# The first superblock's first product done with plain weights, and the combined weights made later

## The chip, the cores and the metric

The kernel runs on one core of a Trainium2 chip. The metric is device time in microseconds: the median of the runs of one build, lower is better. PE is the matrix engine, DVE, ACT and POOL are the vector, scalar and GpSimd engines, and SP issues all DMAs here.

## The reference

Two attentions, then two feed-forward layers over 4608 tokens of width 512, all in fp32. Inner width is 2048.

```python
x = attention(q, packed, packed)            # 4608 x 512, packed = attention(p, k, v)
h = x @ moe_w_in                            # first layer: 512 -> 2048
g = P(h) / (Q(h) + 1e-6)                    # a rational function with |h|
x = g @ moe_w_out                           # 2048 -> 512
h = x @ moe2_w_in                           # second layer: 512 -> 2048
g = h - np.tanh(h)
return g @ moe2_w_out                       # 2048 -> 512
```

## The kernel before

Each fp32 operand of a product is split into a high and a low part (the high part a copy rounded to fp32r, the low part the difference), and a product takes three passes: high x low, low x high, high x high. The weights arrive as 64-bit words and are turned into fp32 on ACT and DVE.

Attention and the first layer run through ten blocks of tokens until about 800 us. The result goes to DRAM as `x2d`. The change concerns the second layer only. There:

- Block 0 (512 tokens) is done plainly. `l3` f (f = 0 to 15) is 12 matmuls 128x512 into one PSUM bank: a slice of 128 of the inner width, from `w3_slot[f]` and the split block `xh`, `xl`. ACT takes tanh (`th`), DVE subtracts (`su`), ACT and DVE split (`yh`, `yl`), and `l4` f adds 12 matmuls with `w4_slot[f]` into four accumulators (f = 15 in four parts, one for each accumulator). Both weights of the layer are loaded during this: a buffer `raw` holds 64-bit words of `w4[f]` and `w3[f + 2]` (two 512 KB loads on SP), DVE and ACT convert them, ACT writes the high part, DVE or POOL the low one. There are two such buffers, so the load for f waits until the conversion for f - 2 is done.
- The other 4096 tokens are four superblocks s = 0 to 3 of 1024 tokens, and these use seven products of half-size blocks in place of eight. The first product of a superblock (`m3`, j = 0 to 7, seven products i of 6 matmuls each, 336 matmuls) needs seven sums or differences of quarters of x (`xa`, and their split `xsh`, `xsl`), and seven combined quarters of the weights. DVE puts its results together (`u2`, `u3`, `h22`, `h21`, `h12`), ACT takes tanh, DVE subtracts (`g11` and so on) and writes the `g` arrays into the slots of `w4`. The second product (`m4`, seven products i of 8 steps, 48 matmuls a product, 336 in all) splits `g` into `yh`, `yl` (`gh` on ACT, `gl` on DVE) for each product.
- The combined weights are made once: for each kind (3 or 4) and j, two sums (`ps`, `prep_sum`), four differences (`pm`, `prep_make`), a split (`ph`, `pl`) into a staging tile `stg` (two of them, which the outputs use too), and a store to DRAM (`pb` stores the three quarters that need no sum, `pd` the four that do). They come back through a ring of four tiles of 8 KB a partition: `load_w3` (`w3d`) and `load_w4` (`w4d`). Two of the ring's tiles are the `raw` buffers, the other two `xh` and `xl` of block 0.

The order is not written out. Every step is entered into a planner (`Plan`) with an engine, a cost, what it needs and a due time, and the planner lists the steps engine by engine. Each engine then runs its list strictly in order, so a step that waits holds up all behind it; that holds for SP's list of DMAs too. A step "EITHER" goes to POOL or DVE.

```python
    order = [(3, j) for j in range(NJ2)] + [(4, j) for j in range(NJ2)]      # L1420
        e = d + (2 * j + 5 if kind == 3 else 2 * j + 14)                     # L1422: due times
        ...
        dma(("pd", kind, j), 128 * 8192, lambda k=kind, j=j: prep_store(k, j), [("pl", kind, j)], e + 0.4)
```

Of the kernel before, what the change touches and what calls it, by code (L numbers as in the profile page):

```python
# [173 lines left out]
def packed_attention_moe_kernel(  # L174
# [555 lines left out]
    w3d = dram_p.tile([NJ2, 128, 7, 2, 256], F32, name="w3d")  # L730
    w4d = dram_p.tile([7, 2, 128, 4, 2, 256], F32, name="w4d")
    x_bufs, xr_t, th_t, yh_t, yl_t, o_t = [], {}, {}, {}, {}, {}
# [6 lines left out]
    def x_load(k):  # L739
        t = yx.tile([128, 512], F32, tag="xr", name="xr", bufs=2)  # L740
        sp.dma_start(out=t, in_=x2d[:, k, 0:NBLK])
        xr_t[k] = t

    def x_high(k):
        act.activation(out=x_bufs[0][:, k, :], in_=xr_t[k], func=AF.Copy)

    def x_low(k, by):
        h, l = x_bufs
        by.tensor_tensor(out=l[:, k, :], in0=xr_t.pop(k), in1=h[:, k, :].bitcast(F32), op=ALU.subtract)

    def hy(f):
        return ps_t[f // 2, "y"][:, f % 2, :]

    def l3(f):
        if f % 2 == 0:
            ring((f // 2, "y"))
        s = w3_slot[f]
        xh, xl = x_bufs
# [7 lines left out]
        for j, (a, b) in enumerate(seq):  # L766
            pe.matmul(out=hy(f), lhsT=a, rhs=b, start=(j == 0), stop=(j == len(seq) - 1))  # L767

    def elem(f, step):
        if step == 0:  # L770
            th_t[f] = yt.tile([128, 512], F32, tag="t", name="t", bufs=TT)
            act.activation(out=th_t[f], in_=hy(f), func=AF.Tanh)
        t = th_t[f]
# [66 lines left out]
    def prep_high(kind, j):  # L840
        s = staged[kind, j] = stg.tile([128, 2048], F32R, tag="stg", name="stg", bufs=2).rearrange(
            "p (part n) -> p part n", part=2)
        act.activation(out=s[:, 0, :], in_=made[kind, j].rearrange("p n f -> p (n f)"), func=AF.Copy)

    def prep_low(kind, j, by):
        s = staged[kind, j]
        by.tensor_tensor(
            out=s[:, 1, :], in0=made[kind, j].rearrange("p n f -> p (n f)"), in1=s[:, 0, :].bitcast(F32), op=ALU.subtract
        )

    def prep_to(kind, j, i):
        if kind == 3:
            return w3d[j][:, ONE.index(i), :, :]
        return w4d[TWO.index(i), j // 4][:, j % 4, :, :]

    def prep_base(kind, j):
        for i, x, half_ in ((1, 0, 0), (2, 0, 1), (3, 1, 1)) if kind == 3 else ((1, 0, 0), (2, 1, 0), (3, 1, 1)):
            s = pair_slot(kind, j, x)[:, 0:1024].rearrange("p (part n) -> p part n", part=2)
            sp.dma_start(out=prep_to(kind, j, i), in_=s[:, :, 256 * half_:256 * half_ + 256].bitcast(F32))

    def prep_store(kind, j):
        s = staged[kind, j]
        for n, i in enumerate(MADE):
            sp.dma_start(out=prep_to(kind, j, i), in_=s[:, :, 256 * n:256 * n + 256].bitcast(F32))

# [3 lines left out]
    def open_ring():  # L869
        ring_w.extend([weights.tile().bitcast(F32R) for _ in range(2)])  # L870
        ring_w.extend(x.rearrange("p k t -> p (k t)") for x in x_bufs)
# [60 lines left out]
    def m3(s, j, i):  # L932
# [128 lines left out]
    add = plan.add  # L1061
# [292 lines left out]
    def open_x():  # L1354
# [3 lines left out]
        x_buf(yx)  # L1358
# [25 lines left out]
    for k in range(4):  # L1384
        e = d - 12 + 2 * k + O("x")
        free = [("xl", k - 2)] if k >= 2 else []
        dma(("xr", k), 512 * 512, lambda k=k: x_load(k), [("open x",)] + reach(0, NBLK) + free, e - 2)
        add(("xh", k), "ACT", c_act(512, 0, 1), lambda k=k: x_high(k), [("xr", k)], e)
        add(("xl", k), EITHER, BOTH, lambda by, k=k: x_low(k, by), [("xh", k)], e, port=True)
# [3 lines left out]

    for f in range(NF):
        e = d + f
        need = [("xl", k) for k in range(4)] if f == 0 else []
# [4 lines left out]
        add(("l3", f), "PE", 12 * MM, lambda f=f: l3(f), need + ago("l3", f, 1), e + P_3, **kw)  # L1401
        add(("th", f), "ACT", AC, lambda f=f: elem(f, 0), [("l3", f), ("open y",)] + ago("yl", f, TT), e + P_E + O("th"))
        add(("su", f), "DVE", AD, lambda f=f: elem(f, 1), [("th", f)], e + P_E)
        add(("yh", f), "ACT", c_act(512, 0, 1), lambda f=f: elem(f, 2), [("su", f)] + ago("l4", f, RING), e + P_E)
        add(("yl", f), "DVE", AD, lambda f=f: elem(f, 3), [("yh", f)], e + P_E, port=True)
# [7 lines left out]
        for m in range(4):  # L1413
# [3 lines left out]
            dma(("os", m), 512 * 512, lambda m=m: o_store(m), [("o", m)], e + P_4)  # L1417


    order = [(3, j) for j in range(NJ2)] + [(4, j) for j in range(NJ2)]  # L1420
    for n, (kind, j) in enumerate(order):
        e = d + (2 * j + 5 if kind == 3 else 2 * j + 14)  # L1422
        was = order[n - 1] if n else None
        after = lambda x: [(x, *was)] if was else []
        have = [("w3" if kind == 3 else "w4", 2 * j + x) for x in range(2)] + [("open y",)]
# [11 lines left out]
        dma(("pb", kind, j), 3 * 128 * 2048, lambda k=kind, j=j: prep_base(k, j), have, e + 0.2)  # L1437
# [3 lines left out]
    def slot_free(kind, f):  # L1441
        return [("l3" if kind == 3 else "l4", f), ("ps", kind, f // 2, f % 2), ("pb", kind, f // 2)]

    add(("ring",), None, 0, open_ring, [("l3", NF - 1)] + [x for y in raw_user[-RAW:] for x in y], 0, behind=raw_next(("ring",)))
    LONG = 28.0
    for s in range(NS):
        base = total + NF + LONG * s
# [3 lines left out]
        for k in range(2):  # L1451
            e = base - 13 + 6 * k
            done = [("xsl", s, i, 0) for i in ONE] if k else last_("xsl", 1, 1) + [("xsl", s - 1, i, 1) for i in ONE] if s else []
            if s == 0 and k == 0:
                done = slot_free(3, 0) + slot_free(3, 1)
            if s == 0 and k == 1:
                done = [("xsl", s, i, 0) for i in ONE]
            dma(("xq", s, k), 2 * 128 * 4096, lambda s=s, k=k: xq_load(s, k), done + reach(T0[s], NSUP), e - 2)
            for n, i in enumerate(XORD):
# [6 lines left out]
                if s == 0:  # L1466
# [5 lines left out]
        for j in range(NJ2):  # L1472
# [175 lines left out]
```

## Time and profile before

| | us |
|---|---|
| median of 3 runs | 1581.49 (1577.44 to 1582.29) |
| profiled execution, its own time | 1585.2 |
| its span, first to last instruction | 1583.4 |
| start of the second layer's first matmul | 781.50 |
| block 0 ends, first superblock starts | 917.38 |
| first superblock's second product starts | 1026.97 |
| second superblock starts | 1109.54 |

The page shows each engine's busy time, then the span in 40 slices of 39.6 us (digits are tenths busy, PEclk is the granted clock of PE in tenths of 2.4 GHz). For this change the second half of the span matters, slices 20 to 28. The stages in the table were read from the timeline of PE; one query gives busy times for each of them. Steps are 1.8 us of the profiled execution outside its span.

### The profile page before, as it was taken

The page shows a single profiled execution, that of the slowest core. Times are in us where ns is not written, and L with a number is a line of the kernel's source. Part 1 is how long each engine was busy: PE and PEld are TensorE (multiplying, and loading weights), DVE is VectorE, ACT ScalarE, POOL GpSimd, SP SyncE. Part 2 cuts the span into 40 slices and gives each one's busy share as a digit, 9 for nine tenths or more (in the row PEclk, how much of TensorE's full clock was granted, in tenths as well). Part 3 has the DMA queues.
Part 4 walks back from the last instruction along what each step waited for, and adds up shares of the span by engine and source line. Part 5 has one row for each costly group of instructions (what it writes and reads, how often), then busy time and mean ns, then how long its engine had stood idle before and what let it go on. Part 6 is the DMA issues. An engine that isn't in the chain of part 4 may idle for free.

```text
span 1583.4 us, 21847 instructions
## 1 busy us (share of the span) xinstructions
PE 1472.3 (93%) x8400; PEld 1196.0 (76%) x8400; DVE 1342.4 (85%) x1738; ACT 887.8 (56%) x1230; POOL 142.7 (9%) x88
## 2 busy tenths in 40 slices
PE   5778999999999999999988766899999999999998
PEld 3657787888888888888966555778778877887787
DVE  4888999999999999999989855997669766967685
ACT  3776676677677676777755522454336433633353
POOL 0101011012110102221111110100000000000000
PEclk9889999999999999999999988999999999999999
DMA  6773313130441213131167999956656755665553
GB/s 239 266 261 142 131 69 124 60 124 31 144 145 61 101 70 117 54 140 67 54 232 244 273 280 295 270 202 231 231 196 227 243 197 192 221 229 187 195 196 142
DMA packets 91575, 272.54 MB, mean 172 GB/s; under 512 B 7888, under 2 KB 46928, under 8 KB 76624
## 3 DMA queue, kind: packets, MB, share of 16 engines
q1 hardware_dynamic: 91472, 271.16, 50.7%
q8 instruction: 66, 1.08, 0.3%
q14 instruction: 37, 0.30, 0.1%
HBM read 218.70 MB, written 52.43 MB: 171 GB/s over the span
## 4 chain that ended last, share of the span: by engine, by line
PE 66%; DVE 18%; DMA 5%; ACT 5%; issue 3%; POOL 1%; SPq 0%; DVEq 0%; ACTq 0%; POOLq 0%
PE acc L964 19%; PE acc L656 16%; PE h L964 15%; PE h L643 9%; PE h L767 2%; DMA raw<-in_w_dram 2%; PE h L509 2%; DVE gh L698 1%; DVE yl L1007 1%; DVE t L685 1%; DVE gl L707 1%; DVE m L704 1%; DVE m L700 1%; DVE t L681 1%; DVE slot L521 1%
## 5 line engine op out<-in xcount | busy, mean ns | idle before, releaser
L643 PE MATMUL h<-ah,slot 128*128 128x320 f32 (+3 forms) x1024 | 214.9, 304 | 1.2 <-DVE slot L521 1.2
L656 PE MATMUL acc<-gh,slot 128*128 128x512 f32 (+1 forms) x800 | 178.0, 376 | 10.9 <-DVE slot L1206 10.4
L656 PEld LDWEIGHTS acc<-gh,slot 128*128 128x128 f32 x800 | 149.5, 195 | 35.7 <-DVE slot L1206 12.2
L643 PEld LDWEIGHTS h<-ah,slot 128*128 128x128 f32 x1024 | 170.7, 193 | 2.6 <-DVE slot L521 1.4
L656 PE MATMUL acc<-raw,slot 128*128 128x512 f32 (+1 forms) x720 | 164.6, 379 | 0.0
L643 PE MATMUL h<-al,slot 128*128 128x192 f32 (+3 forms) x512 | 151.1, 309 | 8.0 <-DVE slot L521 2.3
L656 PEld LDWEIGHTS acc<-raw,slot 128*128 128x128 f32 x720 | 130.2, 188 | 31.8 <-issue 10.5
L1003 ACT ACTIVATE yh<-slot 128x512 fp32r<-128x512 f32 x140 | 87.3, 631 | 79.7 <-PE acc L964 31.2
L678 POOL TENSOR_TENSOR m<-u,r 128x1024 f32<-128x1024 f32 (+1 forms) x33 | 72.5, 2198 | 483.4 <-ACT r L674 381.9
L1007 DVE TENSOR_TENSOR yl<-slot,yh 128x512 fp32r<-128x512 f32 x140 | 95.6, 691 | 21.7 <-ACT yh L1003 20.7
L643 PEld LDWEIGHTS h<-al,slot 128*128 128x128 f32 x512 | 98.4, 192 | 18.0 <-DVE slot L521 2.6
L670 ACT ACTIVATE u<-h 128x1024 f32<-128x1024 f32 (+1 forms) x80 | 74.6, 932 | 60.4 <-PE h L643 60.1
L986 ACT ACTIVATE t<-slot 128x512 f32<-128x512 f32 x60 | 37.9, 632 | 110.6 <-DVE slot L979 65.2
L964 PE MATMUL h<-slot,raw 128*128 128x512 f32 x336 | 81.5, 398 | 18.8 <-DVE slot L981 15.6
L681 DVE TENSOR_TENSOR t<-t,h 128x1024 f32<-128x1024 f32 (+1 forms) x80 | 88.3, 1106 | 9.1 <-ACT t L666 8.8
L666 ACT ACTIVATE t<-h,coa 128x1024 f32<-128x1024 f32 (+1 forms) x80 | 89.4, 1120 | 11.2 <-PE h L643 6.3
L656 PE MATMUL acc<-gl,slot 128*128 128x384 f32 (+1 forms) x400 | 93.0, 374 | 2.1 <-DVE gl L707 2.0
L685 DVE SCALAR_TENSOR_TENSOR t<-t,coa,h 128x1024 f32<-128x1024 f32 (+1 forms) x80 | 93.3, 1166 | 1.9 <-ACT u L670 1.2
L690 ACT ACTIVATE r<-m,lnb 128x1024 f32<-128x1024 f32 (+1 forms) x60 | 63.6, 1059 | 53.2 <-POOL m L678 36.8
L964 PEld LDWEIGHTS h<-slot,raw 128*128 128x128 f32 x336 | 63.1, 190 | 35.8 <-DVE slot L981 16.1
L964 PE MATMUL acc<-yh,raw 128*128 128x512 f32 x288 | 88.8, 389 | 0.0
L656 PEld LDWEIGHTS acc<-gl,slot 128*128 128x128 f32 x400 | 71.3, 190 | 21.4 <-issue 8.2
(192 smaller groups left out, 3255.0 us busy)
## 6 DMA issues: line engine op xcount, KB each, us to landing
raw<-in_w_dram SPq DMA_DIRECT2D x64, 512.0 KB, 5.4
w<-w1d SPq DMA_DIRECT2D x28, 1024.0 KB, 4.8
raw<-w4d SPq DMA_DIRECT2D x28, 1024.0 KB, 4.9
raw<-w3d SPq DMA_DIRECT2D x16, 1024.0 KB, 5.3
xh<-w3d SPq DMA_DIRECT2D x16, 1024.0 KB, 5.1
xh<-w4d SPq DMA_DIRECT2D x14, 1024.0 KB, 4.8
xl<-w4d SPq DMA_DIRECT2D x14, 1024.0 KB, 5.3
raw<-w3d SPq DMA_DIRECT2D x16, 768.0 KB, 4.4
```

The source lines that it names most:

```text
L643: pe.matmul(out=ps[:, f, t], lhsT=x, rhs=y, start=(i == 0), stop=(i == len(seq) - 1))
L656: pe.matmul(out=acc_t[n][m][:, 0:XW[n]], lhsT=w2_slot[2 * p + f][:, o:o + 128], rhs=x[:, f, :], start=(p == 0 and part == 512 and f == 0), ...
L666: act.activation(out=t_t[g], in_=hv(g), func=AF.Identity, scale=a3, bias=a2)
L670: act.activation(out=u_t[g], in_=hv(g), func=AF.Abs)
L678: by.tensor_tensor(out=q_m[g], in0=u_t.pop(g), in1=r_t[g], op=ALU.mult)
L681: dve.tensor_tensor(out=t_t[g], in0=t_t[g], in1=hv(g), op=ALU.mult)
L685: dve.scalar_tensor_tensor(out=t, in0=t, scalar=a1, in1=hv(g), op0=ALU.add, op1=ALU.mult)
L690: act.activation(out=r, in_=q_m[g], func=AF.Ln, scale=2.0 ** -LN_SHIFT, bias=lnb[:, 0:1])
L964: pe.matmul(out=to, lhsT=a, rhs=b, start=(first and n == 0 and i in (1, 6, 7, 5)), stop=(last and n == len(seq) - 1), skip_group_check=True,)
L986: act.activation(out=t, in_=b["a"] if what == "t11" else g_of(what[1:], j), func=AF.Tanh)
L1003: act.activation(out=yh_t[s, i, f], in_=g_of(GSRC[i], f), func=AF.Copy)
L1007: by.tensor_tensor(out=yl_t[s, i, f], in0=g_of(GSRC[i], f), in1=yh_t[s, i, f].bitcast(F32), op=ALU.subtract)
```

## The change

Of the first superblock, the first product is now done plainly: `l3` runs for three blocks b = 0, 1, 2 of 512 tokens (b = 1 and 2 are the two halves of superblock 0). For b = 1 and 2, `su` writes straight into the `g` arrays (`g11`, `g12`, `g21`, `g22`; free once the weights of that slot are used, summed and stored), and only `s3` is left of the putting together. Block 1's split x takes the two `raw` buffers, block 2's takes those of block 0. The second product `m4` of superblock 0 stays as it was. Its combined weights (kind 4) are made first, but not before `w4[14]` is there, from j = 1 on not before `w4[15]`; the weights for `m3` (kind 3) follow, and are first used by superblock 1. `w3d` is a plain row of 3584 words a partition in the order 1, 2 (high then low of the pair), 6, 7, 5, 4, 3: stored with rows of 4 KB (the first slot), 8 KB (the four made) and twice 1 KB, in 3 DMAs a j where there were 7. The staging tile holds high and low of one quarter side by side, so the four stores of kind 4 have rows of 2 KB where they had twice 1 KB. The loads of the ring are chained in their order of use (`stream`).

```diff
-    w3d = dram_p.tile([NJ2, 128, 7, 2, 256], F32, name="w3d")
+    w3d = dram_p.tile([NJ2, 128, 3584], F32, name="w3d")
...
-    def x_buf(where):
-        x_bufs.extend(where.tile([128, 4, 512], F32R, tag=f"x{x}0", name=f"x{x}0") for x in "hl")
+    def x_buf(b):
+        if b == 1:
+            x_bufs[b] = [weights.tile().bitcast(F32R).rearrange("p (k t) -> p k t", k=4) for _ in range(2)]
+        else:
+            x_bufs[b] = x_bufs[0] if b else [yx.tile([128, 4, 512], F32R, tag=f"x{x}0", name=f"x{x}0") for x in "hl"]
...
         if step == 1:
-            dve.tensor_tensor(out=t, in0=hy(f), in1=t, op=ALU.subtract)
-            if f % 2:
-                ps_t.pop((f // 2, "y"))
+            to = g_of(f"{b}{f % 2 + 1}", f // 2) if b else t
+            dve.tensor_tensor(out=to, in0=hy(b, f), in1=t, op=ALU.subtract)
...
+    def prep_store(kind, j):
+        s = staged[kind, j].bitcast(F32)
         if kind == 3:
...
+            sp.dma_start(out=w3d[j][:, 1024:3072], in_=s.rearrange("p n part f -> p (n part f)"))
+            return
         for n, i in enumerate(MADE):
...
+    IN_W3 = {1: (0, 0, 512), 2: (0, 256, 768), 6: (0, 1024, 1280), 7: (0, 1536, 1792),
+             5: (1, 0, 256), 4: (1, 512, 768), 3: (1, 1024, 1280)}
...
+    def base_free(b, f):
+        x = f - f % 2 + b - 1
+        return [("l4", x), ("ps", 4, x // 2, 0), ("ps", 4, x // 2, 1), ("pb", 4, x // 2, x % 2)]
...
+    for b in range(1, 3):
+        for f in range(NF):
+            e = d + (16.5 if b == 1 else 24.5) + 0.5 * f
...
+            add(("l3", b, f), "PE", 12 * MM, lambda b=b, f=f: l3(b, f), need, e, **kw)
...
+            add(after_su(b, f), "DVE", AD, lambda b=b, f=f: elem(b, f, 1), [("th", b, f)] + base_free(b, f), e + 0.5)
...
-    order = [(3, j) for j in range(NJ2)] + [(4, j) for j in range(NJ2)]
+    AFTER, LATE = 14, 8
+    order = [(4, j) for j in range(NJ2)] + [(3, j) for j in range(NJ2)]
     for n, (kind, j) in enumerate(order):
-        e = d + (2 * j + 5 if kind == 3 else 2 * j + 14)
+        e = d + (2 * j + 5 if kind == 4 else j + 24)
...
-        have = [("w3" if kind == 3 else "w4", 2 * j + x) for x in range(2)] + [("open y",)]
+        have = [("w3" if kind == 3 else "w4", 2 * j + x) for x in range(2)] + [("w4", min(NF - 1, 2 * j + AFTER) if kind == 4 else NF - 1)] + [("open y",)]
...
-        for j in range(NJ2):
+        for j in range(NJ2) if s else ():
             e = base + 1.75 * j
```

What this does to the lists, at three places. First SP, from the last store of x of the first layer on. Before (`raw<-in_w_dram` are the weight loads, `slot<-x2d` loads x for superblock 0, `w3d<-` are stores of combined weights):

```order
L720 DMA x2d<-q 128x2x384 x2
L859 DMA w3d<-slot_88 128x2x256 x2
L859 DMA w3d<-slot_89 128x2x256
L326 DMA raw<-in_w_dram 128x512
L892 DMA slot_6882<-x2d 128x1024
L892 DMA slot_6883<-x2d 128x1024
L864 DMA w3d<-stg 128x2x256 x4
L326 DMA raw<-in_w_dram 128x512 x2
L859 DMA w3d<-slot_90 128x2x256 x2
```

After, from the same store on (`xr` are the two tiles through which block 1's x is loaded):

```order
L720 DMA x2d<-q 128x2x384 x2
L326 DMA raw<-in_w_dram 128x512 x18
L863 DMA w4d<-slot_74 128x2x256
L863 DMA w4d<-slot_75 128x2x256 x2
L326 DMA raw<-in_w_dram 128x512
L871 DMA w4d<-stg 128x512 x4
L863 DMA w4d<-slot_955 128x2x256
L863 DMA w4d<-slot_1084 128x2x256
L744 DMA xr<-x2d 128x512 x2
```

Eighteen weight loads now stand in one piece; the stores of combined weights begin behind them. Second PE, at the end of block 0. Before, the last `l4` (into `acc`) and then `m3` of superblock 0, whose weights are in `raw`:

```order
L797 MATMUL acc_6899<-yl,ex_6817 128x512
L798 MATMUL acc_6899<-yh,ex_6817 128x512
L799 MATMUL acc_6899<-yh,ex_6817 128x512
L964 MATMUL h<-slot_7038,raw 128x512 x2
L964 MATMUL h<-slot_7305,raw 128x512 x2
```

After, `l4` of f = 13 and then `l3` of block 1, whose x is in `raw` (slot_88 holds w3[0]):

```order
L800 MATMUL acc_6891<-yl,ex_6819 128x512
L801 MATMUL acc_6891<-yh,ex_6819 128x512
L802 MATMUL acc_6891<-yh,ex_6819 128x512
L770 MATMUL h<-raw,slot_88 128x512 x12
L770 MATMUL h<-raw,slot_89 128x512 x12
```

All 16 of block 1 and two of block 2 stand ahead of `l4` of f = 14; the last six matmuls of `l4` stand behind block 2. Third DVE, early in `m4` of superblock 0. Before (`yl<-` is `gl`, L999 are sums of `g`, L906 and L918 belong to x of superblock 1):

```order
L918 TENSOR_TENSOR slot_7253<-slot_6883,slot_7253 128x512
L1007 TENSOR_TENSOR yl<-slot_7663,yh 128x512
L999 TENSOR_TENSOR slot_7663<-slot_7663 128x512
L999 TENSOR_TENSOR slot_7677<-slot_7663,slot_7677 128x512
L1007 TENSOR_TENSOR yl<-slot_7772,yh 128x512
```

After (L833, L841 and L850 are `ps`, `pm` and `pl` of kind 3):

```order
L1020 TENSOR_TENSOR yl<-slot_7930,yh 128x512
L833 TENSOR_TENSOR s_8288<-slot_70 128x512
L850 TENSOR_TENSOR stg<-made,stg 128x4x256
L833 TENSOR_TENSOR s_8303<-slot_71 128x512
L1020 TENSOR_TENSOR yl<-slot_7965,yh 128x512
L841 TENSOR_TENSOR made<-s_8303,s_8288 128x256
```

The making of the last combined weights of kind 3 has moved in between the splits of `g`.

## Rows read from the trace of the kernel before

**Rows 1.** The page: span, PE, and its slices of granted clock and DMA share.

```profile
span 1583.4 us, 21847 instructions
PE 1472.3 (93%) x8400; PEld 1196.0 (76%) x8400; DVE 1342.4 (85%) x1738; ACT 887.8 (56%) x1230; POOL 142.7 (9%) x88
...
PEclk9889999999999999999999988999999999999999
DMA  6773313130441213131167999956656755665553
```

**Rows 2.** Busy times by stage of the second layer, with the columns in the first line.

```profile
core 0: us, PE busy (x) PEld busy (x) DVE busy (x) ACT busy (x) POOL busy (x), PEclk, DMA share, GB/s
781.50:809.73 28.23, 21.42 (x106) 18.60 (x105) 22.51 (x26) 17.73 (x25) 4.66 (x4) 0.98 0.49 169
809.73:917.38 107.65, 89.54 (x336) 68.57 (x336) 97.61 (x149) 55.80 (x81) 16.08 (x14) 0.91 0.88 273
917.38:1026.97 109.59, 84.22 (x337) 65.73 (x337) 71.85 (x115) 36.02 (x56) 13.44 (x14) 0.88 0.94 278
1026.97:1109.54 82.57, 78.92 (x337) 64.09 (x336) 67.87 (x110) 41.01 (x69) 0.00 (x0) 0.98 0.62 220
1109.54:1583.40 473.86, 468.25 (x2017) 376.78 (x2015) 352.59 (x556) 195.59 (x328) 0.00 (x0) 1.00 0.59 204
```

**Rows 3.** Timeline of PE: start, length, instruction, idle time before it and what ended it.

```profile
809.73 0.77 PE L767 MATMUL h<-xh,slot 128*128 128x512 f32 x1 [6.28 <-DVE t L775]
...
818.05 0.39 PE L797 MATMUL acc<-yl,slot 128*128 128x512 f32 x1
...
932.57 0.80 PE L964 MATMUL acc<-slot,xh 128*128 128x512 f32 x1 [4.88 <-DVE o L810]
...
992.42 2.93 PE L964 MATMUL h<-slot,raw 128*128 128x512 f32 x6 [15.64 <-DVE slot L981]
...
1036.22 0.47 PE L964 MATMUL h<-yl,xl 128*128 128x512 f32 x1 [3.65 <-DMA xl<-w4d]
```

**Rows 4.** Timeline of SP's queue, weight loads and what stands between them.

```profile
796.71 0.81 SPq L326 DMA_DIRECT2D raw<-in_w_dram  x2
...
807.88 0.62 SPq L326 DMA_DIRECT2D raw<-in_w_dram  x1
811.15 1.03 SPq L892 DMA_DIRECT2D slot<-x2d  x2
...
819.19 1.00 SPq L326 DMA_DIRECT2D raw<-in_w_dram  x2
...
852.34 0.82 SPq L326 DMA_DIRECT2D raw<-in_w_dram  x2
...
860.19 0.82 SPq L326 DMA_DIRECT2D raw<-in_w_dram  x2
```

**Rows 5.** Timelines of ACT and POOL: first and last step of one buffer's conversion.

```profile
801.64 1.18 ACT L350 ACTIVATE raw<-raw 128x1024 f32<-128x1024 f32 x1 [5.75 <-DMA raw<-in_w_dram]
...
806.26 1.29 POOL L1206 TENSOR_TENSOR slot<-raw,slot 128x512 fp32r<-128x512 f32 x1 [2.73 <-DVE slot L1206]
```

**Rows 6.** Timeline of DVE where it runs without a gap.

```profile
1002.90 1.23 DVE L847 TENSOR_TENSOR stg<-made,stg 128x1024 fp32r<-128x1024 f32 x1
1004.04 0.69 DVE L979 TENSOR_TENSOR ex<-acc,u 128x512 f32<-128x512 f32 x1
1004.64 0.68 DVE L981 TENSOR_TENSOR ex<-acc,u 128x512 f32<-128x512 f32 x1
...
1006.43 0.42 DVE L838 TENSOR_TENSOR made<-s 128x256 f32<-128x256 f32 x1
1006.77 0.69 DVE L983 TENSOR_TENSOR ex<-acc,u 128x512 f32<-128x512 f32 x1
```

**Rows 7.** DMA view of 824 to 832 us, where only combined weights are stored.

```profile
DMA packets 2792, 2.93 MB, mean 367 GB/s; under 512 B 170, under 2 KB 2711, under 8 KB 2792
```

More of the change, by code (lines that the diff above doesn't have):

```diff
@@ L841, in prep_high @@
         s = staged[kind, j] = stg.tile([128, 2048], F32R, tag="stg", name="stg", bufs=2).rearrange(
[L842 to L843 removed]
+            "p (n part f) -> p n part f", n=4, part=2)
+        act.activation(out=s[:, :, 0, :], in_=made[kind, j], func=AF.Copy)
     def prep_low(kind, j, by):
         s = staged[kind, j]
[L847 to L849 removed]
@@ L851, in prep_to @@
-    def prep_to(kind, j, i):
-        if kind == 3:
[L853 to L859, printed above, removed]
@@ L861, in prep_store, with prep_base @@
-    def prep_store(kind, j):
-        s = staged[kind, j]
+        by.tensor_tensor(out=s[:, :, 1, :], in0=made[kind, j], in1=s[:, :, 0, :].bitcast(F32), op=ALU.subtract)
+    def prep_base(kind, j, x):
+        s = pair_slot(kind, j, x)[:, 0:1024].bitcast(F32)
+        if kind == 3 and x == 0:
+            sp.dma_start(out=w3d[j][:, 0:1024], in_=s)
+            return
+        s = s.rearrange("p (part n) -> p part n", part=2)
+        for i, half_ in [(3, 1)] if kind == 3 else [(2, 0), (3, 1)] if x else [(1, 0)]:
+            if kind == 3:
+                to = w3d[j][:, 3072:3584].rearrange("p (part n) -> p part n", part=2)
+            else:
+                to = w4d[TWO.index(i), j // 4][:, j % 4, :, :]
+            sp.dma_start(out=to, in_=s[:, :, 256 * half_:256 * half_ + 256])
@@ L863, in prep_store @@
+    def prep_store(kind, j):
+        s = staged[kind, j].bitcast(F32)
+        if kind == 3:
+            sp.dma_start(out=w3d[j][:, 1024:3072], in_=s.rearrange("p n part f -> p (n part f)"))
+            return
         for n, i in enumerate(MADE):
-            sp.dma_start(out=prep_to(kind, j, i), in_=s[:, :, 256 * n:256 * n + 256].bitcast(F32))
+            sp.dma_start(
+                out=w4d[TWO.index(i), j // 4][:, j % 4, :, :].rearrange("p a f -> p (a f)"),
+                in_=s[:, n, :, :].rearrange("p a f -> p (a f)"),
+            )
@@ L1357, in open_x @@
         yx = pool_of(last, "yx", side="right")
-        x_buf(yx)
+        x_buf(0)
     def open_y():
@@ L1383, in packed_attention_moe_kernel @@
     d = total
[L1384 to L1389, printed above, removed]
+    add(("open x", 1), None, 0, lambda: x_buf(1), [x for y in raw_user[-RAW:] for x in y], 0, behind=raw_next(("open x", 1)))
@@ L1394, in packed_attention_moe_kernel @@
     for f in range(NF):
         e = d + f
-        need = [("xl", k) for k in range(4)] if f == 0 else []
+        need = [("xl", 0, k) for k in range(4)] if f == 0 else []
         need += [("w3", f)]
@@ L1436, in packed_attention_moe_kernel, with stream @@
             [("ph", kind, j)], e + 0.3, port=True)
-        dma(("pb", kind, j), 3 * 128 * 2048, lambda k=kind, j=j: prep_base(k, j), have, e + 0.2)
+        for x in range(2):
+            dma(("pb", kind, j, x), (1 + (x if kind == 4 else 1 - x)) * 128 * 2048, lambda k=kind, j=j, x=x: prep_base(k, j, x), have, e + 0.2 + x * LATE)
         dma(("pd", kind, j), 128 * 8192, lambda k=kind, j=j: prep_store(k, j), [("pl", kind, j)], e + 0.4)
     def slot_free(kind, f):
-        return [("l3" if kind == 3 else "l4", f), ("ps", kind, f // 2, f % 2), ("pb", kind, f // 2)]
-    add(("ring",), None, 0, open_ring, [("l3", NF - 1)] + [x for y in raw_user[-RAW:] for x in y], 0, behind=raw_next(("ring",)))
+        return [("l3", 2, f) if kind == 3 else ("l4", f), ("ps", kind, f // 2, f % 2), ("pb", kind, f // 2, f % 2)]
     LONG = 28.0
+    streamed = []
+    def stream(name, *a, **kw):
+        dma(name, *a, take="w", behind=streamed[-1:], **kw)
+        streamed.append(name)
     for s in range(NS):
-        base = total + NF + LONG * s
+        base = total + NF + (LONG * s + 2 if s else 0)
         last_ = lambda x, *k: [(x, s - 1, *k)] if s else []
-        for k in range(2):
+        for k in range(2) if s else ():
             e = base - 13 + 6 * k
[L1453 to L1456, printed above, removed]
+            if k:
                 done = [("xsl", s, i, 0) for i in ONE]
+            else:
+                done = [("xsl", s - 1, i, 1) for i in ONE] if s > 1 else slot_free(3, 0) + slot_free(3, 1)
             dma(("xq", s, k), 2 * 128 * 4096, lambda s=s, k=k: xq_load(s, k), done + reach(T0[s], NSUP), e - 2)
@@ L1569, in packed_attention_moe_kernel @@
                     if i in (7, 5):
-                        need += [(x, s, NJ2 - 1) for x in ("g11", "u2", "h21", "h12")]
+                        need += [(x, s, NJ2 - 1) for x in ("g11", "u2", "h21", "h12")] if s else [("o", m) for m in range(4)]
                     need += {2: [("mp1", s, 0), ("mp1", s, 1)], 4: [("mu3", s, 0), ("mu3", s, 1)],
```

138 lines of the change are left out of this document (78 added, 60 removed).

## The prediction

> **What bounds the kernel now.** I read the page first. PE is busy 93% of the span, so in general the kernel is bound by PE; but its granted clock dips from 9 to 8 tenths, after the kernel's first slices, only in the 24th and 25th, and the DMA share in the 23rd to 26th is 9 tenths where it is 5 to 7 nearly all the time behind [rows 1]. That is the stretch the change touches. The table by stage then shows what a matmul costs when nothing disturbs PE: 473.86 us for the 2016 matmuls of superblocks 1 to 3, or 0.235 us each, at a granted clock of 1.00 (the upper level, 2.4 GHz) [rows 2]. Against this price the stages of the change lose time. `m3` of superblock 0 takes 109.59 us where 336 x 0.235 = 79.0 would do; the rest of block 0 (809.73 to 917.38) loses about 35 us in the same way; `m4` takes 82.57 and loses 3.6 [rows 2]. So there are about 66 us ahead of 1026.97 that are not matmul work.
>
> The timeline of PE says what ends these waits: 4.88 us for an `o` copy on DVE, 15.64 us for a `u` or `h` result on DVE at 992.42, 3.65 us for a ring load at the start of `m4` [rows 3]. DVE is busy 97.61 of 107.65 us in block 0 [rows 2]: it makes the combined weights there, the `raw` conversions and the elementwise work. The DMA runs at shares of 0.88 and 0.94, 273 and 278 GB/s, in the two stages [rows 2]. So block 0 and `m3` are bound by DVE and by transfers, in turns, and PE waits at a granted clock of 0.91 and 0.88, below full. From 1109.54 on nothing waits.
>
> **The change part by part.** I use the profiled execution: its time is 1585.2 us, and the median of the runs is 1581.49, 3.7 less. The stretch to price runs from 818.05, where PE does the first matmul of `l4` of f = 0 [rows 3], to 1109.54.
>
> *Loads of the weights.* Stores and loads of x leave the front of SP's list, and eighteen 512 KB loads stand in one piece. Before, the third pair did not go out together: one load at 807.88, the second at 819.19 behind `x2d` and stores [rows 4]. What sets the pace now is the buffer: load issued at 796.71, conversion from 801.64 on ACT, low part done on POOL at 806.26 + 1.29 = 807.55 [rows 4, 5], so 10.8 us a buffer and, with two buffers, 5.4 us a pair. PE needs two groups of 12 for each f, 2 x 12 x 0.235 = 5.64 us. Both are about the same, so PE becomes the pace. Block 1's first group stands behind `l3` of f = 15 and `l4` of f = 13. From 818.05 that is 24 groups (14 of `l4`, 10 of `l3`), 24 x 12 x 0.235 = 67.7 us: `l3` of block 1 starts at 885.7. The other bound is the pace of before, 852.34 to 860.19 = 7.85 us a pair [rows 4]; five to six more pairs at 2.2 us above 5.64 put this point at about 899. I take 885.7, since the stores that slowed the pace have left SP's list there.
>
> *Matmuls.* Superblock 0's first product has 2 x 16 x 12 = 384 matmuls in place of 336. The 48 more cost 48 x 0.235 = 11.3 us, all on PE's path. Two groups of `l4` (24 matmuls) also lie behind 885.7. (384 + 24) x 0.235 = 95.9 us.
>
> *Waits in this stretch.* The sums `xa`, the splits `xsh` and `xsl`, the results `u2` to `h12` of superblock 0 and their 15.64 us wait go. What is late next: DVE still makes all of kind 4 while PE runs `l3`. `su` may write a `g` array only after the kind 4 store of that slot has read it, so a `g` waits for SP and DMA. Per j, kind 4 puts 7 x 2 x 128 x 256 x 4 B = 1.835 MB on the queues; at before's 278 GB/s this takes 6.6 us against the 5.64 in which PE does one pair of `l3`. With eight j this is at most 8 x 1 = 8 us, and PSUM and `t` tiles take up a part. I take 4 us, with 0 to 12 as bounds: 0 if the stores keep up, 12 if the last store also delays the loads of `m4`.
>
> *Handing over to `m4`.* The last `l4` and `s3`, `gh`, `gl` stand ahead of the first matmul. Before, PE waited 3.65 us for a ring load here [rows 3]. I take 2.5, bounds 1.5 to 5.
>
> *`m4` of superblock 0.* It took 82.57 us with DVE busy 67.87 [rows 2]. DVE now also makes the combined weights of kind 3 there, and loses nothing in return except copies that went earlier. I count 116 steps on half-tiles, 12 on quarters and 4 splits of 128x1024. In the gapless stretch one step starts 0.60 us after another for 128x512, 0.34 us for 128x256 and 1.14 us for the split (1004.04 to 1004.64; 1006.43 to 1006.77; 1002.90 to 1004.04) [rows 6]. 116 x 0.60 + 12 x 0.34 + 4 x 1.14 = 78.3 us. PE needs 336 x 0.235 = 79.0. I leave 82.6 as before; bounds 79 and 90 (the full durations 0.69, 0.42 and 1.23 [rows 6] give 90).
>
> *Transfers.* From 861, where the last weights of w4 that the stores wait for are converted, to the end of `m4`: 14.7 MB of stores of kind 4, 14.7 of kind 3, 14.7 of loads of kind 4, 3.7 of x for block 2 and superblock 1, 1.0 of output, 0.5 of the last `raw`, 3.7 for the first loads of kind 3: 53.0 MB. To finish by 1070.7 they need 253 GB/s. The two stages before got 273 and 278 [rows 2], so this is covered, by little.
>
> *Longer rows.* Kind 3 goes out in 3 DMAs a j where there were 7. With 0.82 us for two issues [rows 4] this saves SP 8 x 4 x 0.41 = 13 us of issuing, but SP has nothing waiting behind it that PE waits for; I count it at nothing, and 13 us late stores if that cover is gone. Whether longer rows move bytes faster is not shown directly. In the stretch where only combined weights are stored, 2,711 of 2,792 packets are under 2 KB and yet 367 GB/s move [rows 7]. The mixed stage has 278 GB/s at a share of 0.94, 296 at full share; the steady stage, which only loads long rows, has 204 at 0.59, 346 at full share [rows 2]. So I put the gain at zero, with 53.0 MB in 153 rather than 179 us (346 against 296 GB/s) as the other end; it would matter only if transfers bound the stretch.
>
> The Trainium skill, "DMA: Bandwidth & Descriptors", section on specifications, says that transfers of 512 B or more run at line rate; by it the longer rows of this change bring nothing. The 367 GB/s with short packets [rows 7] agree with it, the 296 against 346 do not clearly. By either, the sum stays as it is.
>
> *The sum.* 885.7 + 95.9 + 4 + 2.5 + 82.6 = 1070.7 for the end of `m4`, against 1109.54: 38.8 us less. Superblocks 1 to 3 keep their 473.9 us. The profiled execution would be 1585.2 - 38.8 = 1546.4, the median 1581.49 - 38.8 = 1542.7.
>
> **The rivals.** *Transfers and loads keep their pace of before.* `l3` of block 1 starts at 899, the stretch waits 8 us, handing over 2.5, and `m4` takes 86 as DVE gets late: 899 + 95.9 + 8 + 2.5 + 86 = 1091.4, a gain of 18, or 1563. For it speaks that DMA shares were 0.88 and 0.94 [rows 2]; against it, that POOL and ACT had room (16 and 56 us of 108 [rows 2]) and the stores moved behind the loads.
>
> *Starved by transfers, slower.* All 53 MB fall in one stretch, loads of `m4` behind the stores on the same list. The point from which it decides is 53.0 MB / (1109.54 - 861) = 213 GB/s. At 190 GB/s the transfers take 279 us, `m4` ends at 1140, and the time is about 1612. The stretch of before with both loads and stores gave 273 [rows 2], so it would need a worse mixture; the steady stage's 204 GB/s is at a share of 0.59 only [rows 2], thus no limit.
>
> *The wait moves (no change).* Kind 3 is made so late that superblock 1 waits for it: each `w3d` row must be stored before it is loaded. Making one j is about 8 steps on DVE, 2 x 0.60 + 4 x 0.34 + 1.14 = 3.7 us; four of eight lie in `m4`. If DVE pushed these behind its `gl` work, superblock 1 would wait for up to 8 x 3.7 = 30 us plus a store and a load, and about 35 of the 38.8 would be given back: 1578. Against it: 78.3 of 82.6 us fit.
>
> **How the numbers follow.** Forecast 0.69, transfers and pace as before 0.22, starved 0.05, wait moves 0.04. The predicted time is the forecast's, 1543. Low: all good bounds (no waits, 1.5, 79.0) give 885.7 + 95.9 + 1.5 + 79 = 1062, a gain of 47, 1534, and as the runs scatter by 4 us, and longer rows could give some, 1528. High: the rival at 1563 and a little above, 1568; all bad bounds together (899 + 95.9 + 12 + 5 + 90 = 1102) would give 1574. What lies outside are the starved and moved cases and the far end of the second. A measurement of this kernel can tell 0.3%, 4.7 us, from no change. Faster by more: 0.91; within: 0.03; slower: 0.06.
>
> **What would show it.** In the profile of the changed kernel: `l3` of block 1 starts near 886, pairs of `raw` loads 5.4 to 5.7 us apart, the granted clock near 1.0 between 818 and 985; `m4` starts near 988 and ends near 1071; DMA at 253 GB/s or more between 861 and 1071; DVE without gaps in `m4`; superblocks 1 to 3 in 158 us each. Wrong it would be if PE waits for `su` (a store too late), for `w4d` at the start of `m4`, or for `w3d` in superblock 1.

## The result, and the profile after

| | before | after |
|---|---|---|
| median, us | 1579.61 (1577.44 to 1582.29, 4 runs) | 1538.57 (1534.80 to 1540.94, 4 runs) |
| profiled execution, span | 1583.4 | 1534.7 |
| `l4` of f = 0 starts | 818.05 | 814.44 |
| `l3` of block 1 starts (before: block 0 ends) | 917.38 | 880.81 |
| `m4` of superblock 0 starts | 1026.97 | 978.69 |
| superblock 1 starts | 1109.54 | 1061.19 |

The ratio is 0.9737, 95% interval 0.9707 to 0.9767: 41.0 us faster. Forecast were 38.8 us less and 1543, with 1528 to 1568 as range.

The page of the changed kernel first, its counterpart is [rows 1]. The fence shows span and PE, then granted clock and DMA share in 40 slices.

```profile
span 1534.7 us, 21747 instructions
PE 1462.3 (95%) x8448; PEld 1194.2 (78%) x8448; DVE 1307.3 (85%) x1690; ACT 878.3 (57%) x1216; POOL 135.2 (9%) x82
...
PEclk8888999999999999999999999999999999999999
DMA  7783314221332303132134696776656655665553
```

PE runs 48 matmuls more than before and is busy 10 us less. The two slices with a clock of 8 tenths in the second half are gone, and only one slice has a DMA share of 9 tenths where there were four. The stages, one row each (rest of block 0; from `l3` of block 1 to `m4`; `m4`; the three other superblocks), with the columns of [rows 2] and against its rows:

```profile
807.48:880.81 73.33, 73.33 (x312) 59.65 (x313) 58.31 (x85) 43.74 (x65) 11.84 (x9) 0.98 0.54 185
880.81:978.69 97.88, 94.21 (x410) 76.35 (x408) 66.20 (x111) 34.12 (x52) 8.83 (x12) 1.00 0.78 263
978.69:1061.19 82.50, 79.64 (x337) 62.44 (x338) 77.75 (x130) 45.70 (x75) 1.30 (x1) 1.00 0.73 269
1061.19:1534.70 473.51, 468.24 (x2017) 376.76 (x2015) 352.45 (x556) 195.42 (x328) 0.00 (x0) 1.00 0.60 207
```

In block 0, PE is busy in every one of the 73.33 us: the 18 us of waits are gone, and the granted clock is 0.98 where it was 0.91. In the second row 3.67 us are idle, in `m4` 2.86, where DVE is now busy 77.75 of 82.50 us. The last row is that of before to 0.4 us. So the whole gain lies in block 0 and the first product, as forecast. PE's timeline has these waits behind 880 us (the two ahead of `m4`; seven more in it, of 0.15 to 0.67 us, make up the 2.86; in brackets the idle time and what ended it):

```profile
935.83 0.50 PE L770 MATMUL h<-xh,slot 128*128 128x512 f32 x1 [1.63 <-DVE ex L779]
978.69 0.50 PE L977 MATMUL h<-yl,raw 128*128 128x512 f32 x1 [2.04 <-DVE yl L1020]
```

The waits of 15.64 and 4.88 us in [rows 3] have no successor.

### The profile page after: what moved, and what is told of

Its sections match the earlier page's. It is cut to its first block, busy times and chain, and to the rows that moved or that the text cites. A ratio compares the mean times of both kernels' runs of the same rounds, so it can differ in the third digit from the quotient of the medians.

```text
span 1534.7 us, 21747 instructions
## 1 busy us (share of the span) xinstructions
PE 1462.3 (95%) x8448; PEld 1194.2 (78%) x8448; DVE 1307.3 (85%) x1690; ACT 878.3 (57%) x1216; POOL 135.2 (9%) x82
## 4 chain that ended last, share of the span: by engine, by line
PE 68%; DVE 21%; ACT 5%; issue 3%; DMA 2%; POOL 1%; SPq 0%; DVEq 0%; ACTq 0%; POOLq 0%
PE acc L977 17%; PE acc L656 16%; PE h L977 12%; PE h L643 9%; PE h L770 9%; DVE yl L1020 2%; PE h L509 2%; DVE t L685 1%; DMA raw<-in_w_dram 1%; DVE gh L698 1%; DVE t L681 1%; DVE gl L707 1%; DVE m L704 1%; DVE m L700 1%; DVE slot L1012 1%
## 5 line engine op out<-in xcount | busy, mean ns | idle before, releaser
L656 PEld LDWEIGHTS acc<-gh,slot 128*128 128x128 f32 x800 | 149.5, 195 | 36.0 <-DVE slot L1219 12.8
L1020 DVE TENSOR_TENSOR yl<-slot,yh 128x512 fp32r<-128x512 f32 x140 | 95.5, 693 | 15.6 <-ACT yh L1016 14.8
L770 PE MATMUL h<-xh,slot 128*128 128x512 f32 x256 | 83.9, 399 | 8.0 <-DVE t L779 6.4
L1016 ACT ACTIVATE yh<-ex 128x512 fp32r<-128x512 f32 x84 | 52.6, 631 | 50.6 <-PE acc L977 25.5
L977 PE MATMUL acc<-yh,raw 128*128 128x512 f32 x256 | 78.9, 389 | 0.0
L999 ACT ACTIVATE t<-slot 128x512 f32<-128x512 f32 x45 | 28.5, 633 | 85.8 <-DVE slot L992 48.8
```

Source lines behind the costliest of these rows:

```text
L656: pe.matmul(out=acc_t[n][m][:, 0:XW[n]], lhsT=w2_slot[2 * p + f][:, o:o + 128], rhs=x[:, f, :], start=(p == 0 and part == 512 and f == 0), ...
L770: pe.matmul(out=hy(b, f), lhsT=a, rhs=w, start=(j == 0), stop=(j == len(seq) - 1))
L977: pe.matmul(out=to, lhsT=a, rhs=b, start=(first and n == 0 and i in (1, 6, 7, 5)), stop=(last and n == len(seq) - 1), skip_group_check=True,)
L1016: act.activation(out=yh_t[s, i, f], in_=g_of(GSRC[i], f), func=AF.Copy)
L1020: by.tensor_tensor(out=yl_t[s, i, f], in0=g_of(GSRC[i], f), in1=yh_t[s, i, f].bitcast(F32), op=ALU.subtract)
```

## The experiments

Stage lengths come from each run's own trace: A from the first `l4` to the first `l3` of block 1, B from there to `m4`, C is `m4`. A of the changed kernel holds 288 matmuls, B 408. In no_hold, plain_early, make_extra and store_extra, 24 matmuls of `l4` (some 5.5 us) stand in A instead of B.

| run | A | B | C | median, us |
|---|---|---|---|---|
| changed kernel | 66.37 | 97.88 | 82.50 | 1538.57 |
| after_again | 66.38 | 97.87 | 82.55 | 1538.26 |
| short_rows | 66.37 | 97.88 | 82.53 | 1539.96 |
| no_hold | 92.30 | 88.49 | 77.78 | 1552.21 |
| plain_early | 89.08 | 110.18 | 77.24 | 1565.76 |
| make_extra | 91.12 | 103.18 | 83.06 | 1568.84 (one run) |
| store_extra | 92.54 | 94.99 | 83.63 | 1564.41 (one run) |
| hold_alone (A to `m3`, B is `m3`) | 78.25 | 142.75 | 83.74 | 1596.37 |
| fewer | 66.34 | 81.84 | 82.52 | 1523.42 |
| double | 66.35 | 110.19 | 82.54 | 1552.61 |
| l4_early | 66.37 | 95.99 | 83.07 | 1538.49 |
| spread | 66.35 | 96.00 | 80.53 | 1534.53 |
| hold12 | 70.60 | 102.54 | 84.02 | 1546.80 |

**The same kernel again.** 

> The changed kernel itself once more, beside the next runs. Time 1535 to 1541 as before. If the 2.3 us by which the first layer ended earlier in the first trace (second layer from 779.2 instead of 781.5) belong to one execution only, this trace shows another start; if the change itself moved the first layer, it shows 779 again.

Ratio 0.9731 (0.9707 to 0.9754). Here the second layer starts at 783.67, in the first trace at 779.20; the stages behind differ by at most 0.05 us. So the stages can be compared to a tenth of a microsecond, while the time of a run cannot: of the 5.0 us between the two profiled executions, 4.5 lie ahead of the second layer.

**Longer rows.** The stores go back to 1 KB rows (`stg` holds high and low apart again), seven DMAs a j:

```diff
-            sp.dma_start(out=w3d[j][:, 1024:3072], in_=s.rearrange("p n part f -> p (n part f)"))
-            return
...
         for n, i in enumerate(MADE):
...
+            sp.dma_start(out=prep_to(kind, j, i), in_=s[:, :, 256 * n:256 * n + 256].bitcast(F32))
```

> The changed kernel with the stores of before: seven DMAs a j with rows of twice 1 KB for both kinds, everything else as in the changed kernel. The prediction's step (longer rows count at nothing): 1536.5 to 1540.5, l3 of block 1 from about 881, m4 ends at about 1061. Rival, rows gave the transfers their room (53 MB in 153 instead of 179 us, 13 us of SP issuing): PE waits for su behind late stores or for the ring loads of m4, 1545 to 1565.

Ratio 0.9741 (0.9718 to 0.9764), and the stages are equal. Stage B of this run, with the columns of [rows 2], is:

```profile
888.00:985.88 97.88, 94.22 (x410) 76.35 (x408) 66.18 (x111) 34.26 (x52) 8.86 (x12) 1.00 0.83 263
```

The same 263 GB/s take a DMA share of 0.83 with short rows and 0.78 with long ones. So long rows do save DMA time, 6% of it here, but nothing waits for it: they are worth nothing in this kernel. The Trainium skill, "DMA: Bandwidth & Descriptors", section on specifications, has all transfers from 512 B on at line rate; for the time of the kernel that came out, for the DMA engines' own share it is not quite so.

**No hold.** Kind 4 is made as soon as its slots are there:

```diff
-... + [("w4", min(NF - 1, 2 * j + AFTER) if kind == 4 else NF - 1)] + [("open y",)]
+... + ([("w4", NF - 1)] if kind == 3 else []) + [("open y",)]
```

> The changed kernel, but kind 4 is made as soon as its own two slots are there, not after w4[14] and w4[15]; its stores stand between the weight loads again. The prediction's step (stores behind the loads let the loads keep PE's pace): pairs of loads 7 to 8 us apart for five to six pairs, l3 of block 1 starts 8 to 14 us later (889 to 895), 1546 to 1553. Rival, the plain product alone took the waits away: l3 of block 1 at 881, 1536 to 1541.

Ratio 0.9815 (0.9791 to 0.9840). The time is where it was expected, 14 us above the changed kernel, but it comes about in another way. A grows by 26 us, 20 without the matmuls that moved there, where 8 to 14 were expected; B is shorter by 9, of which 5.5 are these matmuls, and C by 4.7: DVE makes no combined weights there, and 12 of its steps on x of superblock 1 fall into `m4` instead of 21. SP's timeline shows where the loads stop (the `raw` loads are the weight loads):

```profile
806.85 2.71 SPq L326 DMA_DIRECT2D raw<-in_w_dram  x3
...
818.28 1.80 SPq L871 DMA_DIRECT2D w4d<-stg  x4
...
830.25 0.81 SPq L326 DMA_DIRECT2D raw<-in_w_dram  x2
```

SP stands for 8 us ahead of a store whose tile is still being made, and no weight load leaves for 20 us. It looks as if the store held up the loads; make_extra below, which has no such store, shows the same pause, so the store is not its cause.

**Plain product alone.** Neither kind is held, and kind 3 is made ahead of kind 4 with the due times of before:

```diff
-    order = [(4, j) for j in range(NJ2)] + [(3, j) for j in range(NJ2)]
+    order = [(3, j) for j in range(NJ2)] + [(4, j) for j in range(NJ2)]
-        e = d + (2 * j + 5 if kind == 4 else j + 24)
+        e = d + (2 * j + 5 if kind == 3 else 2 * j + 14)
...
-        have = [... for x in range(2)] + [("w4", min(NF - 1, 2 * j + AFTER) if kind == 4 else NF - 1)] + [("open y",)]
+        have = [... for x in range(2)] + [("open y",)]
```

> The plain product alone: the changed kernel, but the combined weights are made in the order and at the due times of before (kind 3 first, then kind 4, each as soon as its slots are there). The theory that the plain product and the later making are both needed: the weight loads go at 7 to 8 us a pair again, and the g arrays of block 1 wait for kind 4, which now comes last; 1550 to 1575. Rival, the plain product alone is the cause: 1537 to 1545.

Ratio 0.9889 (0.9868 to 0.9910). A is 3 us shorter than in no_hold, and B now has 13.94 us of PE waits, nearly all for `su` (5.83 and 4.11 us the longest), which stands on DVE behind the making of kind 4 or waits for a store of it to leave a `g` slot. C is 77.24 us, with no wait at all. The plain product without the new order is worth 1.1%, that is 17 of the 41 us.

**Later making alone.** The kernel before, with the hold:

```diff
-        have = [... for x in range(2)] + [("open y",)]
+        have = [... for x in range(2)] + [("w4", min(NF - 1, 2 * j + 14) if kind == 3 else NF - 1)] + [("open y",)]
```

> The later making alone: the kernel before, with its m3 of superblock 0, but kind 3 is not made before w4[14] or w4[15] is there and kind 4 not before w4[15]. Block 0 then ends near 892 instead of 917, but m3 of superblock 0 waits for kind 3: its first load comes only after the first making and a store, and DVE has sums, splits, results and the making in it. The theory that moving needs the plain product as cover: what block 0 gains m3 gives back, 1570 to 1600. Rival, moving alone is the cause: 1540 to 1558.

Ratio 1.0079 (1.0056 to 1.0102), 0.8% slower. Block 0 gets 21 us shorter (78.25 against 99.33), and `m3` 33 us longer. In PE's timeline, then ACT's:

```profile
909.91 2.07 PE L964 MATMUL h<-slot,raw 128*128 128x512 f32 x4 [14.14 <-DVE slot L918]
...
947.03 1.22 PE L964 MATMUL h<-slot,raw 128*128 128x512 f32 x2 [33.15 <-DVE slot L918]
```

```profile
944.06 1.06 ACT L843 ACTIVATE stg<-made 128x1024 fp32r<-128x1024 f32 x1 [23.80 <-DMA out_dram<-o]
```

PE waits for the split of x (L918). The first of the two splits waits for a load of x that SP issues only at 899.96, among the stores of kind 3. The second stands behind the making, which waits 23.80 us for a staging tile: block 0's output, held in it, is stored by SP behind some thirty stores that the hold had let go together. So this order of the lists is slow; a better one for the same idea was not tried.

**Making or storing.** What in the early making stretches A? Two runs took it apart. In make_extra kind 4 is made once more in block 0 (as a kind 5, into the same tiles), and nothing of it is stored:

```diff
-    order = [(4, j) for j in range(NJ2)] + [(3, j) for j in range(NJ2)]
+    order = [(5, j) for j in range(NJ2)] + [(4, j) for j in range(NJ2)] + [(3, j) for j in range(NJ2)]
```

> What stretched block 0 when kind 4 was made early (92.3 us from the first l4 to l3 of block 1 instead of 66.4, 5.5 of it for two groups of l4 more): the making itself on DVE, ACT and POOL, or its stores. Here the changed kernel makes kind 4 once more in block 0, as soon as the slots are there, and stores nothing of that; the weight loads stay in one piece on SP's list. If the making alone did it: 75 to 87 us from the first l4 to l3 of block 1. If the stores did it, by their bytes or by standing ahead of loads in SP's list: 66 to 69.

In store_extra seven pieces of each pair of slots are stored to a spare place, and nothing is made:

```diff
+    for j in range(NJ2):
+        dma(("extra", j), 7 * 128 * 2048, lambda j=j: extra_store(j), [("w4", 2 * j), ("w4", 2 * j + 1)], d + 2 * j + 5)
```

> The counterpart: the changed kernel stores seven 256 KB pieces of each pair of w4 slots to a spare place in block 0, as soon as the slots are there, 14.7 MB in all, without any making. The stores stand between the weight loads, but wait for no making. If bytes or queue places are what stretched block 0: 75 to 87 us from the first l4 to l3 of block 1. If it takes stores that wait for the making ahead of loads on SP's list: 66 to 70.

Each alone stretches A about as much as both together: 91.12 and 92.54 against 92.30. Both expectations that left one of them out fell. A of no_hold, of make_extra, then of store_extra:

```profile
818.79:911.09 92.30, 79.49 (x313) 62.22 (x312) 71.42 (x111) 46.41 (x67) 13.76 (x12) 0.93 0.78 250
```

```profile
816.13:907.25 91.12, 78.32 (x311) 61.31 (x309) 69.86 (x107) 45.24 (x66) 14.65 (x12) 0.94 0.36 123
```

```profile
817.90:910.44 92.54, 78.41 (x314) 61.64 (x313) 55.00 (x72) 39.68 (x59) 13.94 (x11) 0.93 0.67 216
```

In no_hold it was the making. In make_extra no store stands between the loads until 878 us, and yet the loads pause for the same 20 us, from 806.6 to 826.89. SP's timeline, and DVE's with the last step of a conversion (the low part, L1219), read:

```profile
803.19 3.40 SPq L326 DMA_DIRECT2D raw<-in_w_dram  x3
...
826.89 20.84 SPq L326 DMA_DIRECT2D raw<-in_w_dram  x8
```

```profile
826.14 1.28 DVE L1219 TENSOR_TENSOR slot<-raw,slot 128x512 fp32r<-128x512 f32 x2
```

The load leaves when the first of these two low parts is done, at about 826.8; in no_hold the same step starts at 829.51 and the load leaves at 830.25, though SP has had nothing to issue since 827.7. PE's longer waits in A are the same one by one too, 1.25, 0.60, 1.79, 2.28, 0.92 and 5.45 us in make_extra, 1.24, 0.60, 1.81, 2.29, 0.92 and 5.45 in no_hold. So in A the stores cost no_hold at most the 1.2 us between the two. The waits of 5.45 us are for a `yl` that stands on DVE behind sums of the making and splits of x, the others for converted weights.

store_extra has a path of its own: its stores stand between the loads and wait for the slots that they store. But not all of its 92.54 us is their price. The load of `w4[15]` leaves at 897.52, behind stores of the first quarters that kind 4 makes itself: SP waits for these from 891.25 to 894.57 and issues them until 897.43, some 6 us in all. In the changed kernel the load leaves ahead of them. PE's longest wait there, 8.23 us, is for these weights. That stores alone cost as much as the making is therefore not shown.

No engine is full in make_extra, and DMA is at 0.36. What is full is the cycle of the two load buffers: load, conversion on ACT and DVE, low part, next load. The first step of a conversion on ACT, for f = 5 and f = 13, in the changed kernel and in make_extra:

```profile
810.91 1.13 ACT L350 ACTIVATE raw<-raw 128x1024 f32<-128x1024 f32 x1
...
854.44 1.17 ACT L350 ACTIVATE raw<-raw 128x1024 f32<-128x1024 f32 x1 [0.32 <-POOL slot L1219]
```

```profile
810.12 1.17 ACT L350 ACTIVATE raw<-raw 128x1024 f32<-128x1024 f32 x1
...
883.30 1.13 ACT L350 ACTIVATE raw<-raw 128x1024 f32<-128x1024 f32 x1
```

That is (854.44 - 810.91) / 8 = 5.44 us a pair of loads, and 9.15 in make_extra. The kernel before has 8.97 by the same rows (818.80 and 890.57), no_hold 8.30, store_extra about 8.0. What was queued between the steps of this cycle, the making on ACT, DVE and POOL or the stores on SP, lengthened it. PE then waits, and runs at a granted clock of 0.93 to 0.94: in no_hold, 12.8 us of A are waits and about 7.6 are matmuls that take longer (79.49 us for 313, against 66.37 for 289).

**What is next to PE.** Four of twelve matmuls are left out of each group of block 1 and 2, so that the result lacks one pass there:

```diff
+        if b:
+            seq = [x for n, x in enumerate(seq) if n % 2 == 0 or n >= 8]
```

> The changed kernel without the pass high x low (xl) in block 1 and 2: four matmuls of each of the 32 groups are left out, 128 in all. If PE is the bound of this stretch, with 0.23 us a matmul, 29 us go: 1508 to 1511. If the transfers set it next (25 MB between 881 and 977, at 296 GB/s 85 us) only about 11 go: 1526 to 1530. If DVE or the waits for stores do, somewhere between.

Ratio 0.9620 (0.9600 to 0.9639), 1523.42: between the bounds for PE and for the transfers, as expected if DVE or the waits for stores come next. B falls by 16 us where PE has 29 us less to do. From 900 to 924 us the row of the changed kernel and of this run are:

```profile
900.00:924.00 24.00, 24.00 (x108) 19.87 (x107) 21.88 (x37) 10.11 (x13) 4.42 (x6) 1.00 1.06 324
```

```profile
900.00:924.00 24.00, 18.40 (x70) 13.79 (x69) 22.59 (x39) 11.30 (x17) 4.65 (x7) 0.93 1.02 307
```

In the changed kernel PE, DVE (21.88 of 24 us) and DMA (share 1.06, 324 GB/s) are all full there. With less on PE, the other two stay full and PE waits for `su` (9.5 us in B; 2.03 more are for the first `yl` of `m4`). This run does not tell which of the two comes next.

**More stores.** The made quarters of kind 4 are stored twice:

```diff
+        for n, i in enumerate(MADE):
+            sp.dma_start(out=w4x[TWO.index(i), j // 4][:, j % 4, :, :]..., in_=s[:, n, :, :]...)
```

> The changed kernel, but each of the 32 stores of the four made quarters of kind 4 is issued twice, the second time to a spare place: 8.4 MB and 32 DMAs more, most of them between 868 and 925. If 296 GB/s is the limit of a mixed stretch, the 33 MB up to 977 take 113 instead of 96 us: 10 to 18 us more, 1549 to 1557. If the transfers have room (367 GB/s in a stretch of stores alone): 0 to 4 us more, 1538 to 1543.

Ratio 0.9805 (0.9785 to 0.9825): B is 12.3 us longer, with 11.4 us of waits, 8.8 of them for `su`. B moves 302 GB/s, more than the 296 that had been worked out as a limit from stages with more loads, and 385 in a part with stores alone (924 to 940). At the 324 GB/s above, 8.4 MB would take 26 us, so about half was hidden. The time fits the first expectation, its limit was somewhat low. The copies also put 32 more issues on SP's list, some 13 us at 0.41 us each, which this run does not part from their bytes; for the bytes speaks that the DMA share is 1.03 from 900 to 924 us and 1.07 from 924 to 940.

**A better order.** In the changed kernel DVE's timeline ahead of `m4` reads:

```profile
976.01 0.69 DVE L813 COPY o<-acc 128x512 f32<-128x512 f32 x1 [3.55 <-PE acc L802]
...
977.95 2.49 DVE L1020 TENSOR_TENSOR yl<-slot,yh 128x512 fp32r<-128x512 f32 x4
```

The splits for `m4` (L1020) stand behind the copy of block 0's output, which waits for the last `l4`; and that output holds a staging tile that the making of kind 3 wants. So the last `l4` was put ahead:

```diff
             need += [("l3", b, f - 1) if f else ("l3", b - 1, NF - 1)]
+            if b == 2 and f == 3:
+                need.append(("l4", NF - 1))
```

> The changed kernel, but all of l4 of f = 15 must be done before the fourth group of block 2, so that the output tile leaves its staging buffer early and the copies don't stand ahead of the splits for m4 on DVE. If the 2.0 us wait at the start of m4 and the 2.9 us of small DVE waits in m4 come from that order, 4 to 5 us go: 1533 to 1535. If they are DVE's own pace: 1537 to 1540.

Ratio 0.9719 (0.9694 to 0.9744), which the times cannot tell from the changed kernel. In the trace the 2.04 us are gone. All of kind 3 but one last split is made ahead of `m4`, so DVE is busy 69.83 us there in place of 77.75; but `m4` is no shorter, since PE now waits 2.41 us for a split that stands behind steps on superblock 1's x. The next run also makes the two loads of that x wait for part of `m4`:

```diff
+            if s == 1:
+                done = done + [("m4", 0, TWO[4 if k else 2], 3)]
             dma(("xq", s, k), 2 * 128 * 4096, ...)
```

> The kernel with all of l4 of f = 15 ahead of block 2's fourth group, in which m4 still waited 2.4 us for yl behind four or five steps on x of superblock 1; here the two loads of that x wait for half of m4's third and fifth product, so that these steps come later. If the remaining waits in m4 are this order on DVE: m4 in 77.5 to 80 us instead of 83.1 and 82.5, time 1533 to 1536. If DVE's load as such sets m4: 82 to 83 us, 1537 to 1539.

Median 1534.53, ratio 0.9701 (0.9687 to 0.9715). B and C are together 3.85 us shorter than in the changed kernel, and the median is 4.0 less. `m4` took 80.53, above the 77.5 to 80 expected; 2.02 us of waits for `yl` are left. Its median is the lowest of the versions that compute everything, but its interval overlaps that of the changed kernel: the stages show the gain, the times alone do not. The last run takes l4_early with a shorter hold, `AFTER = 12`:

> All of l4 of f = 15 early as before, and kind 4 of j = 0 held for w4[12] only, j = 1 for w4[14], the others for w4[15]: between no hold (1552) and the hold of the changed kernel (1538). If the loads suffer already when two stores of the making come ahead of the last pairs: block 0 2 to 5 us longer, 1538 to 1543. If the last pairs have slack and DVE gains in block 1 and 2 what it then need not do in m4: block 0 66 to 67 us, m4 78 to 80, 1533 to 1536.

Ratio 0.9782 (0.9766 to 0.9799), slower than either expectation. A is longer by matmuls that moved there, with no wait. B has a wait of 9.37 us: the copy of the output stands on DVE 8.82 us ahead of its `l4`, with `su` and the making behind it. That is this order of DVE's list, and says nothing of the length of a hold.

## Why the prediction was right

- **The pace of the loads** (5.4 us a pair, so PE's 5.64 decides) was right: 5.44, and no PE wait from 807.48 to 935. The 24 groups took 66.37 us instead of 67.7: a matmul costs 66.37 / 288 = 0.2305 us there. The 0.235 was a mean over superblocks 1 to 3 that held idle time of its own (468.25 of 473.86 us busy in [rows 2], 0.2323 a matmul without it). The reason given, that the stores had slowed the pace and have left SP's list, was only part of it: make_extra has hardly a store between the loads and yet 9.15 us a pair. The hold helps because it moves the making as well.
- **What was to be won** was read somewhat too high. By the prediction's own price the 107.65 us of 809.73 to 917.38 lose 107.65 - 336 x 0.235 = 28.7 us, not 35; the 6.28 us that PE waits just before make up the rest. The sum does not use it.
- **The bound of the other side** was too low. The pace of before was taken from two issues, 7.85 us [rows 4]; over eight pairs it is 8.97. The rival of kept paces was priced at 13 us in block 0; no_hold shows 20, given back in part later, which the rival did not have.
- **408 matmuls and 4 us of waits, then 2.5**: 102.4 forecast, 97.88 measured, 94.21 of it PE's work and 3.67 waits (1.63 and 2.04). For the waits on stores, taken as 4 us, none is seen: the 1.63 us are for an `su` that DVE runs right behind steps of the making. The 2.04 us were near the 2.5 by luck, for the cause was another: not a ring load, but the split behind the output's copy (l4_early takes it away). The ring wait of before, 3.65 us at 1036.22 [rows 3], is not at the start of `m4` (1026.97) but inside it, so the sum had it twice, in the 2.5 and in the 82.6.
- **`m4`** was forecast at 82.6 and took 82.50. The sum for DVE (78.3) came to 77.75. But the equal time was luck, it hid an exchange: the 3.65 us ring wait went, and 2.86 us of waits for `yl` came, with slower first matmuls behind each wait. Without any making in `m4`, no_hold and plain_early take 77.78 and 77.24. But l4_early, with one step of it left, takes 83.07, so the making alone is not what costs the 5 us. The first two also have fewer steps on superblock 1's x in `m4` (12 and 4, where the changed kernel has 21 and l4_early 22), and spread, with these later, takes 80.53. The order of DVE's list there decides; how the 5 us divide is open.
- **Transfers covered, by little**: 253 GB/s needed; 263 and 269 moved in B and C, 258 over the whole of 861 to 1061. double agrees with the "little".
- **Longer rows at nothing**: right for the time, with the DMA share down by 0.05.
- **The whole sum** came out at 1070.7 for the end of `m4` against 1061.19. Of these 9.5 us, 3.6 lie ahead of the stretch (814.44 against 818.05; the second trace has 819.40, so mostly one execution's scatter), 1.3 in A, 4.5 in B, 0.1 in C. From the second layer's first matmul to the end the two traces of the changed kernel are 46 us shorter than that of before, the medians 41. The profiled execution of before was 2 to 6 us above the medians of its kernel; where it lost them, one trace can't tell. So the stages gained some 6 us more than forecast (1.3, 4.5 and 0.1), and that the median came as near to the 38.8 as 41.0 is in part luck.

More stores do stretch B (double), but at 53 MB the starved rival did not come about. The rival of a moved wait did not happen: superblock 1 starts without one.

The theory that both halves of the change are needed stands on four runs: plain product alone 17 us faster, with kind 4 made first but not held 29 (no_hold), with the hold 41; later making alone (in the one order tried) 14 us slower.

## What to carry to other kernels

Where loads go round a few buffers, count the cycle of one buffer (load, every conversion step, release), not the bytes: what is put between its steps in an in-order list can lengthen it, here 5.44 us to 8 or 9, and the cure here was to keep other work off those lists until the last load was nearly there. To find out which list it is, leave the work in one list and take it out of the other: the store ahead of which SP stood looked guilty, and was not. A stage in which no engine and no DMA is full can still be full in this sense. Compare stages of traces rather than whole times where an early part of the kernel scatters.

## Not expected of the hardware

The stores cost the stretch of loads next to nothing on top of the making: with the making alone A took 91.12 us and moved 123 GB/s, with the stores as well 92.30 at 250 GB/s. Part of a wait's price is paid behind it: of the 20 us in no_hold, 7.6 were not waits but slower matmuls. Behind PE's waits of 1.81 and 5.45 us there, the granted clock was 0.51 (877.20 to 880.40) and 0.50 (906.40 to 911.00), that is its lower level of 1.2 GHz, and matmuls started 0.43 us apart, not 0.23.
